# Linear attention followed by a routed expert network: third tiles for the attention, later weights for the second expert, and another order of the steps

## The chip, the core and the metric

The kernel runs on one core of a Trainium2 chip. A core has a matrix engine (PE, with a weight-load queue PEld beside it), a vector engine (DVE), an activation engine (ACT), a general engine (POOL) and a queue engine (SP) that here only issues DMAs. POOL also issues DMAs, among them those that change the number type on the way. The five run their own instruction streams in order and wait for each other by semaphores. The metric is device time in microseconds (us): the median of repeated executions of the whole program, from the inputs in device memory to the output in device memory.

## The reference

```python
def _attn_ref(q, k, v, w_phi):                 # q, k, v: 8 x 8 x 576 x 64
    def phi(x):
        proj = np.einsum('bhsd,df->bhsf', x, w_phi)            # 64 -> 128
        proj = proj - np.max(np.abs(proj), axis=-1, keepdims=True)
        return np.concatenate([np.exp(proj), np.exp(-proj)], axis=-1)
    q_p, k_p = (phi(q), phi(k))
    kv = np.einsum('bhsf,bhsd->bhfd', k_p, v)
    z = np.sum(k_p, axis=2)
    num = np.einsum('bhsf,bhfd->bhsd', q_p, kv)
    den = np.einsum('bhsf,bhf->bhs', q_p, z)[..., None] + 1e-06
    return num / den
# x = the heads side by side: 4608 rows of 512

def _moe_ref(x, w_gate, w1, w2):               # 8 experts, 512 -> 1024 -> 512
    logits = x @ w_gate
    P = np.exp(logits - logits.max())
    for _ in range(8):
        P /= P.sum(1, keepdims=True) + 1e-09
        P /= P.sum(0, keepdims=True) + 1e-09
        P *= N / E
    out = 0
    for e in range(E):
        out += P[:, e:e + 1] * (np.maximum(x @ w1[e], 0.0) @ w2[e])
    return out
```

Every row goes through all eight experts; only the weights P differ by row. P needs the column sums over all 4608 rows, so it can't be formed before the attention is done.

## The kernel before

**Attention.** The eight batches have eight heads each, taken as four pairs of heads, so there are 32 pairs; of each head's 576 rows, 512 are done pair by pair and the last 64 ("rests") for a whole batch at once. A pair goes through four steps. Step a (`pair_a`): the keys stand transposed in a tile `qkT`, PE multiplies them by the small matrix `wphi` (scores), DVE takes the row maxima (`m`, L459), ACT takes the exponentials of both signs (`k0`, `k1`, L463), and POOL scales v by the exponentials of the maxima (`v0`, `v1`, L592). Step q: the same for the queries (`q0`, `q1`). Step b (`pair_b`): PE forms the key-value product, DVE copies it out of PSUM (`kv`, L647), PE multiplies the query features by it in two halves, with a DVE product between them (L678), and DVE divides (reciprocal `rec`, L684, and the products into `xb`, L686 and L691). Step c (`pair_c`): PE transposes `xb` (L705) and DVE copies it into `xT` (L708). Steps r and g do the rests (L479, L525, L720, L725) and the gate's logits of a batch. For the first two batches q and k arrive as 32-bit numbers in the tiles `acc` by way of SP (L389), and PE transposes them (L544); for the others POOL issues a DMA that casts to 16 bits (L395) and SP a DMA that transposes (L412).

**First expert under the attention.** A group is 512 rows of x; there are nine. Step u multiplies a group by two slices of the first expert's `w1` (`up0`, PE L467, ACT evicts with a relu at L759), eight matrix products of 512 columns each. Step d multiplies by `w2` (`down0`), eight products too, and copies into `acc` (L794 on ACT, L801 on DVE). Neither needs P yet, so they fill PE between the attention's short products. Groups 5 to 8 have their `acc` tiles only once the attention's memory has been given back, so their d steps come behind it.

**Handover.** When the last attention tile has been read, the memory of the attention's tiles is released (the plan's key `late`) and used for `acc5` to `acc8`, for the routing and for the experts' sums. DVE then runs eight rounds of the routing (L929 to L946, with a small PE product with `colw` in each round) between the differences of x (`S`, L987) that go out to device memory (`xd`) and come back as `X`. PE meanwhile does what is left of the first expert. When P is there, ACT scales all 36 tiles of the first expert's result by it (L1241).

**The other seven experts** use a scheme with seven products in place of eight on 2 x 2 blocks (PE L1079; ACT L1107, L1116, L1231; DVE L1111, L1219, L987; POOL L1234). Their weights are loaded by POOL (L361) into rings of two tiles each, cast on the way.

**What sets the order.** Nothing is issued directly: every instruction is recorded in a `Plan` with a cost, and a list scheduler places them on the engines, the earliest start first, and among equals the one recorded first. The costs are estimates in `pe`, `act`, `dve`, `pool`, `dma`, the tiles come from rings (`ring(pool, shape, type, name, count)`) and the eight PSUM banks from `Banks`; an instruction can't be placed before a tile of its ring is free. The string `order` gives the order in which the attention's steps are recorded (each letter is the next one of its kind). What the scheduler returns is the order that each engine's stream has on the chip.

Of the kernel before, what the change touches and what calls it, by code (L numbers as in the profile page):

```python
# [9 lines left out]
FP32 = mybir.dt.float32  # L10
# [218 lines left out]
def kernel(  # L229
# [19 lines left out]
    NJ = 4  # L249
# [28 lines left out]
    wgate_f = a_in.tile([128, NP, E], FP32, name="wgate_f")  # L278
# [35 lines left out]
    ring(wp, [128, 4, FF], BF16, "w1", 2)  # L314
    ring(wp, [128, 8, DD], BF16, "w2", 2)
# [11 lines left out]
    ring(a_s, [128, 2, 8], FP32, "m", 2)  # L327
    ring(a_s, [128, 12], FP32, "r", 2)
    ring(a_s, [128, 6], FP32, "rec", 3)
    ring(a_s, [128, NP, 128], BF16, "xb_r", 2)  # L330
    for x in range(2):
        ring(a_t, [128, NP, DF], BF16, f"kr{x}", 2)
        ring(a_t, [128, NP, 128], BF16, f"qr{x}", 2)
        ring(a_t, [128, 8, DF], BF16, f"k{x}", 2)
        ring(a_t, [128, 2, 4, 128], BF16, f"q{x}", 2)
        ring(a_t, [128, 8, D1], BF16, f"v{x}", 2)
        ring(a_s, [128, NP], FP32, f"em_r{x}", 2)
        ring(a_s, [128, 8], FP32, f"em{x}", 2)
# [27 lines left out]
    def load_w0(i, r):  # L366

        w1, w2 = W[0]
        n = i % 4
        if i < 4:  # L370
            dma("POOL", 1 << 19, 250, lambda: nc.gpsimd.dma_start(
                out=w1()[:, :, n * 256:(n + 1) * 256],
                in_=moe_w1[0].rearrange("(c p) f -> p c f", p=128)
                [:, :, n * 256:(n + 1) * 256]), r, [(w1, n)])
        else:
            dma("POOL", 1 << 19, 280, lambda: nc.gpsimd.dma_start(
                out=w2()[:, 2 * n:2 * n + 2, :],
                in_=moe_w2[0].rearrange("(c p) f -> p c f", p=128)
                [:, 2 * n:2 * n + 2]), r, [(w2, n)])

    def load_qk(b, hh, nh, t, r=()):

        o = hh % 4
        keys = [o // 2] if nh == 2 else [0, 1]
        if b < 2:
            g = t["f"]
            for x, src in ((1, k), (0, q)):
                i = 2 * x + o // 2
                dma("SP", nh << 17, 320, lambda x=x, src=src, i=i: nc.sync.dma_start(  # L389
                    out=acc[g][:, i:i + nh // 2].rearrange("p a (h c) -> p (a h) c", h=2),  # L390
                    in_=src[b, hh:hh + nh, 0:SM].rearrange("h (p j) d -> p h (j d)", j=NJ)),
                    r, [("acc", g, 2 * x + n) for n in keys])
            return
        for x, src in ((1, k), (0, q)):
            dma("POOL", nh << 17, 230, lambda x=x, src=src: nc.gpsimd.dma_start(  # L395
                out=t["qk"]()[:, x, o:o + nh],
                in_=src[b, hh:hh + nh, 0:SM].rearrange("h (p j) d -> p h (j d)", j=NJ)),
                r, [(t["qk"], x, i) for i in keys])

    def load_v(b, hh, nh, t, r=()):  # L400
        o = hh % 4
        keys = [o // 2] if nh == 2 else [0, 1]
        dma("SP", nh << 17, 320, lambda: nc.sync.dma_start(
            out=t["v"]()[:, o:o + nh],
            in_=v[b, hh:hh + nh, 0:SM].rearrange("h (p j) d -> p h (j d)", j=NJ)),
            r, [(t["v"], i) for i in keys])
# [24 lines left out]
    def load_rests(b0, nb, r=()):  # L431
# [3 lines left out]
        for h in range(2):  # L435
# [6 lines left out]
            for x, src in ((1, k), (0, q)):  # L442
# [6 lines left out]
                dma("POOL", nb << 16, 90, lambda rows=rows, x=x, src=src, part=part:  # L449
# [19 lines left out]
    def rest_a(b, t):  # L469
# [6 lines left out]
        if b < 2:  # L476
            ptr = new("P1")
            for pr in range(NP):
                pe(128, lambda pr=pr: nc.tensor.transpose(  # L479
# [3 lines left out]
                    [ptr, ("acc", 0, b)])  # L483
# [50 lines left out]
    def pair_a(b, pr, t):  # L534
# [3 lines left out]
        if b < 2:  # L538
            g = t["f"]
            for x in (1, 0):  # L540
                ptr = new("P1")
                i = 2 * x + h0 // 2
                for c in range(4):
                    pe(128, lambda c=c, i=i, ptr=ptr: nc.tensor.transpose(  # L544
                        ptr()[:, c * 128:(c + 1) * 128], acc[g][:, i, c * 128:c * 128 + 128],
                        identf), [("acc", g, i), "identf"], [ptr])
# [75 lines left out]
    def pair_b(b, pr, s, r):  # L622
# [29 lines left out]
        def outs(h):  # L652
# [8 lines left out]
            def feats(x):  # L661
# [3 lines left out]
                for j in range(4):  # L665
# [3 lines left out]
                        skip_group_check=True), keys, [pn])  # L669
# [137 lines left out]
    for b in range(2):  # L807
# [18 lines left out]
    load_qk(0, 4, 4, halves[0, 1])  # L826
    load_v(0, 4, 4, halves[0, 1])
    for i in range(2):
# [4 lines left out]
    dma("SP", 1 << 14, 50, lambda: nc.sync.dma_start(  # L833
        out=wgate_f, in_=moe_w_gate.rearrange("(c p) e -> p c e", p=128)), w=["wgate_f"])
    act(32, lambda: nc.scalar.copy(out=wgate, in_=wgate_f), ["wgate_f"], ["wgate"])

# [29 lines left out]
    def stage_g(b):  # L866
# [8 lines left out]
        "raqaqabbccqaqbbaqrbaccuqrbgaqaquabcucbqccaruqbcabqdaqbacbugdqdaqubdccuubauacuqqd"  # L875
        "drcbagubqbdaqrduabccauqccubqdcbcuadgqgrbuadqbacaudqbqaddcbaurqcuqbcaadubqauabdqd"
        "gbuccdaqdqbdcbqcuuacbgcqcbcg"
# [407 lines left out]
    for e in range(1, E):  # L1285
        w1, w2 = load_w(e, [("xT", 5, 3)])
# [50 lines left out]
```

## Time and profile before

| | |
|---|---|
| median of 3 runs | 1040.92 us (1040.34 to 1041.95) |
| the profiled execution | 1041.77 us, of which the span is 1040.0 us |
| PE busy | 1014.6 us (98%) |
| DVE busy | 821.6 us (79%) |
| ACT busy | 711.6 us (68%) |
| POOL busy | 462.2 us (44%) |
| start, until the first pair's `kv` is copied | 0 to about 21.5 us |
| attention with the first expert under it | to about 216.5 us |
| the rest of the first expert, and the routing | to 259.8 us |
| the seven other experts | to the end |

Times are counted from the first instruction of the span. Busy times of PE, DVE and ACT include the tail of an instruction that overlaps the next one, so back-to-back instructions follow each other more closely than the mean duration of one says. A group's row names the line, the engine, the operation and the tiles with their numbers left out, and behind the bar the idle time of the engine just before these instructions with what ended it.

### The profile page before, as it was taken

The page shows a single profiled execution, that of the slowest core. Times are in us where ns is not written, and L with a number is a line of the kernel's source. Part 1 is how long each engine was busy: PE and PEld are TensorE (multiplying, and loading weights), DVE is VectorE, ACT ScalarE, POOL GpSimd, SP SyncE. Part 2 cuts the span into 40 slices and gives each one's busy share as a digit, 9 for nine tenths or more (in the row PEclk, how much of TensorE's full clock was granted, in tenths as well). Part 3 has the DMA queues.
Part 4 walks back from the last instruction along what each step waited for, and adds up shares of the span by engine and source line. Part 5 has one row for each costly group of instructions (what it writes and reads, how often), then busy time and mean ns, then how long its engine had stood idle before and what let it go on. Part 6 is the DMA issues. An engine that isn't in the chain of part 4 may idle for free.

```text
span 1040.0 us, 24497 instructions
## 1 busy us (share of the span) xinstructions
PE 1014.6 (98%) x9473; PEld 842.0 (81%) x9512; DVE 821.6 (79%) x1626; ACT 711.6 (68%) x1570; POOL 462.2 (44%) x532
## 2 busy tenths in 40 slices
PE   6889999999999999999999999999999999999998
PEld 4556666654788888888888888888888888888886
DVE  6999999988777787778876877788777877787675
ACT  7999999945976666666666665666666656666663
POOL 3886775500234444444434444344444444434442
PEclk9999999999999999999999999999999999999999
DMA  8999979534411161113311441134111611114333
GB/s 240 161 186 144 156 122 173 88 142 112 82 43 51 41 125 50 42 42 83 82 42 42 92 89 45 42 70 99 48 42 48 127 42 42 42 46 128 114 131 122
DMA packets 105237, 93.94 MB, mean 90 GB/s; under 512 B 45344, under 2 KB 80288, under 8 KB 105120
## 3 DMA queue, kind: packets, MB, share of 16 engines
q1 hardware_dynamic: 71840, 68.45, 24.2%
q0 software_dynamic: 33120, 23.86, 16.5%
q8 instruction: 74, 1.21, 0.5%
q14 instruction: 43, 0.35, 0.1%
q10 hardware_dynamic: 160, 0.07, 0.0%
HBM read 94.98 MB, written 14.16 MB: 105 GB/s over the span
## 4 chain that ended last, share of the span: by engine, by line
PE 89%; ACT 3%; DVE 3%; DMA 3%; issue 1%; SPq 0%; DVEq 0%; ACTq 0%
PE P L1079 71%; PE P L467 16%; ACT acc L1241 2%; DMA acc<-in_q_dram 1%; DMA qkT<-qk 1%; PE P L666 1%; DVE m L459 1%; ACT V L1231 1%; PE P L705 1%; ACT U L1107 0%; SPq L389 0%; DVE xb L686 0%; ACT hT L1116 0%; DVE P L678 0%; PE P L671 0%
## 5 line engine op out<-in xcount | busy, mean ns | idle before, releaser
L1234 POOL TENSOR_TENSOR acc<-acc,V 128x512 f32<-128x512 f32 x248 | 317.4, 1287 | 441.0 <-ACT V L1231 437.5
L1111 DVE CUSTOM_DVE_ANT_0 hT<-P,U 128x512 bf16<-128x512 f32 x378 | 255.4, 688 | 129.9 <-ACT U L1107 81.4
L1107 ACT COPY U<-P 128x512 f32<-128x512 f32 x378 | 217.4, 590 | 125.4 <-PE P L1079 120.9
L1231 ACT ACTIVATE V<-P 128x256 f32<-128x256 f32 x496 | 205.8, 476 | 134.7 <-PE P L1079 123.5
L1079 PEld LDWEIGHTS <-w 128*128 128x128 bf16 x2016 | 197.2, 98 | 24.3 <-issue 1.2
L1079 PEld LDWEIGHTS <-S 128*128 128x128 bf16 x1984 | 194.1, 98 | 23.1 <-issue 0.6
L1219 DVE SCALAR_TENSOR_TENSOR acc<-P,acc 128x256 f32<-128x256 f32 x372 | 159.3, 478 | 54.4 <-PE P L1079 51.9
L1079 PEld LDWEIGHTS <-T 128*128 128x128 bf16 x1512 | 147.9, 98 | 18.5 <-issue 1.4
L1079 PEld LDWEIGHTS <-hT 128*128 128x128 bf16 x1488 | 145.4, 98 | 18.2 <-DVE hT L1111 1.1
L1079 PE MATMUL P<-X,w 128*128 128x256 bf16 x1008 | 154.8, 273 | 0.4 <-ACT U L1107 0.4
L1079 PE MATMUL P<-xT,w 128*128 128x256 bf16 x1008 | 151.2, 273 | 0.4 <-ACT acc L794 0.4
L1079 PE MATMUL P<-X,T 128*128 128x256 bf16 x1008 | 148.5, 273 | 0.7 <-ACT U L1107 0.7
L1079 PE MATMUL P<-w,hT 128*128 128x256 bf16 x992 | 142.5, 273 | 0.6 <-DVE hT L1111 0.6
L1079 PE MATMUL P<-T,S 128*128 128x256 bf16 x1056 | 136.3, 273 | 0.4 <-ACT V L1231 0.4
L1079 PE MATMUL P<-w,S 128*128 128x256 bf16 x928 | 126.8, 273 | 0.0
L592 POOL TENSOR_TENSOR v<-v_m,em 128x512 bf16<-128x512 f32 x64 | 66.7, 1042 | 66.1 <-ACT em L463 49.0
L459 DVE TENSOR_REDUCE m<-P 128x4 f32<-128x512 f32 x128 | 83.7, 680 | 4.3 <-PE P L467 2.6
L1116 ACT ACTIVATE hT<-P 128x512 bf16<-128x512 f32 x126 | 73.7, 604 | 12.5 <-PE P L1079 11.9
L987 DVE TENSOR_TENSOR S<-hT 128x1024 bf16<-128x1024 bf16 x124 | 80.2, 683 | 0.0
L467 PE MATMUL P<-w,hT 128*128 128x512 bf16 x301 | 77.6, 379 | 1.2 <-DVE m L459 0.2
L1079 PE MATMUL P<-xT,T 128*128 128x256 bf16 x504 | 75.8, 273 | 0.0
L467 PE MATMUL P<-xT,w 128*128 128x512 bf16 x270 | 73.3, 379 | 1.1 <-DVE m L459 0.2
(94 smaller groups left out, 1088.1 us busy)
## 6 DMA issues: line engine op xcount, KB each, us to landing
X<-xd SPq DMA_DIRECT2D x126, 256.0 KB, 2.6
w<-in_moe_w_dram POOLq DMA_DIRECT2D x14, 1024.0 KB, 10.1
v_m<-in_v_dram SPq DMA_DIRECT2D x15, 512.0 KB, 5.3
out_dram<-acc SPq DMA_DIRECT2D x14, 512.0 KB, 2.9
xd<-S SPq DMA_DIRECT2D x18, 256.0 KB, 2.1
qk<-in_k_dram POOLq DMA_DIRECT2D x12, 256.0 KB, 5.2
qk<-in_q_dram POOLq DMA_DIRECT2D x12, 256.0 KB, 6.2
w<-in_moe_w_dram POOLq DMA_DIRECT2D x8, 256.0 KB, 7.0
```

Of the source, the lines that this page charges most:

```text
L459: dve(el, lambda: nc.vector.tensor_reduce(out=dst(), in_=src(), axis=AX.X, op=ALU.max, apply_absolute_value=True), r, w)
L467: nc.tensor.matmul(out_, lhsT=lhsT, rhs=rhs, start=start, stop=stop)
L592: pool(512, lambda y=y, em=em: nc.gpsimd.tensor_tensor(out=s["v"][y]()[:, :, 0:D], in0=t["v"]()[:, h0:h0 + 2].rearrange("p a (b c) -> p (a ...
L987: lambda: f.tensor_tensor(out=out_(), in0=x(), in1=y(), op=op), r, w, **kw)
L1079: pe(256, lambda i=i, k=k, z=z: nc.tensor.matmul(bank()[:, 256 * i:256 * i + 256], lhsT=lhs(k, i), rhs=rhs(k), start=first and z, stop=k = ...
L1107: act(512, lambda: nc.scalar.copy(out=u[fp][n]().rearrange("p a b -> p (a b)"), in_=x[fp]()), [x[fp]], [u[fp][n]])
L1111: dve(500, lambda: nc.vector._custom_dve(ADD_SAT, out=out_(fp, i, j), in0=bank[fp]().rearrange("p (a b) -> p a b", a=2), in1=u[fp][n](), s ...
L1116: act(512, lambda: nc.scalar.activation(out=out_(fp, i, j), in_=x[fp]().rearrange("p (a b) -> p a b", a=2), func=ACT.Relu, bias=0.0, scale ...
L1219: dve(330, lambda n=n, ts=ts: nc.vector.scalar_tensor_tensor(out=acc[g][:, ts, 256 * j:256 * j + 256], in0=bank()[:, 256 * n:256 * n + 256 ...
L1231: act(390, lambda n=n: nc.scalar.activation(out=u()[:, n, :], in_=bank()[:, 256 * n:256 * n + 256], func=ACT.Copy, bias=0.0, scale=P[:, 4 ...
L1234: pool(670, lambda: nc.gpsimd.tensor_tensor(out=acc[g][:, 2 * i:2 * i + 2, 256 * j:256 * j + 256], in0=acc[g][:, 2 * i:2 * i + 2, 256 * j: ...
L1241: act(512, lambda ts=ts: nc.scalar.activation(out=acc[g][:, ts, :], in_=acc[g][:, ts, :], func=ACT.Copy, bias=0.0, scale=P[:, 4 * g + ts, ...
```

## The change

It has five parts.

1. **Third tiles.** The rings of the attention's tiles `rT`, `qkT`, `kv`, `m`, `r`, `k0`, `k1`, `q0`, `q1`, `v0`, `v1`, `em0`, `em1` have three tiles in place of two, and `xb` four in place of three. The input rings (`qk`, `v_m`, `qk_r`, `v_r`) keep two.
2. **The second weights' place and time.** The second tile of `w1` and of `w2` lies in the memory that the attention gives back. So the weights of the second expert are loaded behind `late`; before, they were loaded once the fourth pair of batch 5 was in `xT`.
3. **Small loads.** The gate's weights are cast by a DMA that POOL issues, in place of a DMA on SP and a cast on ACT. One of the two copies of `w_phi` is loaded by POOL, not ACT. The loads of batch 0's second half are cut in two, in the order k, q, v of heads 4 and 5, then of heads 6 and 7.
4. **The planner's numbers.** DMA rates are lower, the 32-bit transposes are costed at 260 columns in place of 128, and some products take tiles of their rings earlier.
5. **Another string `order`.**

Parts 1, 2, 4 and 5 change no instruction's work; they move instructions. By the two orders, 378 of the first expert's 576 products stood ahead of the last transpose of `xb` on PE before, and 361 stand there now.

The core of the diff:

```diff
@@ -310,33 +310,35 @@
-    ring(wp, [128, 4, FF], BF16, "w1", 2)
-    ring(wp, [128, 8, DD], BF16, "w2", 2)
+    for tag, shape in (("w1", [128, 4, FF]), ("w2", [128, 8, DD])):
+        ring(wp, shape, BF16, tag, 2)
+        R[tag].make = lambda i, w, tag=tag, shape=shape: (late["s_p"] if i else wp).tile(
+            shape, BF16, name=tag, tag=f"{tag}_{i}")
...
-    ring(a_t, [128, NP, 128], BF16, "rT", 2)
-    ring(a_t, [128, 2, 8, 128], BF16, "qkT", 2)
-    ring(a_t, [128, 2, 2, D1], BF16, "kv", 2)
-    ring(a_t, [128, NJ, 128], BF16, "xb", 3)
+    ring(a_t, [128, NP, 128], BF16, "rT", 3)
+    ring(a_t, [128, 2, 8, 128], BF16, "qkT", 3)
+    ring(a_t, [128, 2, 2, D1], BF16, "kv", 3)
+    ring(a_t, [128, NJ, 128], BF16, "xb", 4)
...
-        ring(a_t, [128, 8, DF], BF16, f"k{x}", 2)
-        ring(a_t, [128, 2, 4, 128], BF16, f"q{x}", 2)
-        ring(a_t, [128, 8, D1], BF16, f"v{x}", 2)
+        ring(a_t, [128, 8, DF], BF16, f"k{x}", 3)
+        ring(a_t, [128, 2, 4, 128], BF16, f"q{x}", 3)
+        ring(a_t, [128, 8, D1], BF16, f"v{x}", 3)
...
-            dma("POOL", 1 << 19, 250, lambda: nc.gpsimd.dma_start(
+            dma("POOL", 1 << 19, 200, lambda: nc.gpsimd.dma_start(
...
-                pe(128, lambda pr=pr: nc.tensor.transpose(
+                pe(260, lambda pr=pr: nc.tensor.transpose(
...
-                        True, True), [(t["T"], 0, h0 // 2), "wphi2"], [pt])
+                        True, True), [(t["T"], 0, h0 // 2), "wphi2"], [pt], own)
...
@@ -808,10 +809,9 @@
-    dma("ACT", 1 << 15, 100, lambda: nc.scalar.dma_start(out=wphi_f[0:64, :], in_=w_phi),
-        w=["wphi_f0"])
-    dma("ACT", 1 << 15, 100, lambda: nc.scalar.dma_start(out=wphi_f[64:128, :], in_=w_phi),
-        w=["wphi_f1"])
+    for i, (queue, eng) in enumerate((("ACT", nc.scalar), ("POOL", nc.gpsimd))):
+        dma(queue, 1 << 15, 100, lambda i=i, eng=eng: eng.dma_start(
+            out=wphi_f[64 * i:64 * i + 64, :], in_=w_phi), w=[f"wphi_f{i}"])
...
-    load_qk(0, 4, 4, halves[0, 1])
-    load_v(0, 4, 4, halves[0, 1])
+    for h0 in (4, 6):
+        load_qk(0, h0, 2, halves[0, 1])
+        load_v(0, h0, 2, halves[0, 1])
+    dma("POOL", 1 << 14, 20, lambda: nc.gpsimd.dma_start(
+        out=wgate, in_=moe_w_gate.rearrange("(c p) e -> p c e", p=128)), w=["wgate"])
...
-    dma("SP", 1 << 14, 50, lambda: nc.sync.dma_start(
-        out=wgate_f, in_=moe_w_gate.rearrange("(c p) e -> p c e", p=128)), w=["wgate_f"])
-    act(32, lambda: nc.scalar.copy(out=wgate, in_=wgate_f), ["wgate_f"], ["wgate"])
...
     order = (
-        "raqaqabbccqaqbbaqrbaccuqrbgaqaquabcucbqccaruqbcabqdaqbacbugdqdaqubdccuubauacuqqd"
...
+        "arqaqaqbaqabccbrbqabrcqccaquubaqagbcubcqucuadqgrbabqacqdcbuadabqbuduqccuabauuqcg"
...
-        w1, w2 = load_w(e, [("xT", 5, 3)])
+        w1, w2 = load_w(e, ["late"])
```

What this does to the streams is shown at three places. In the rows a name left of the arrow is what an instruction writes, P is PSUM, and the lines of the changed kernel are off by one or so from those above.

DVE at the start, from the second pair's cast of the transposed keys to the first pair's `kv` copy, before:

```order
L548 CAST qkT<-P 128x512
L484 CAST rT<-P 128x512
L459 TENSOR_REDUCE m<-P 128x4 x2
L459 TENSOR_REDUCE m_r<-P 128x4 x2
L459 TENSOR_REDUCE m<-P 128x4 x2
L548 CAST qkT<-P 128x512 x4
L647 CAST kv<-P 128x260
```

and in the changed kernel:

```order
L549 CAST qkT<-P 128x512
L485 CAST rT<-P 128x512
L460 TENSOR_REDUCE m<-P 128x4
L460 TENSOR_REDUCE m_r<-P 128x4
L460 TENSOR_REDUCE m<-P 128x4
L460 TENSOR_REDUCE m_r<-P 128x4
L460 TENSOR_REDUCE m<-P 128x4 x2
L549 CAST qkT<-P 128x512 x2
L460 TENSOR_REDUCE m<-P 128x4 x2
L549 CAST qkT<-P 128x512 x2
L648 CAST kv<-P 128x260
```

Ahead of the first `kv` copy stand two row maxima (`m`) more, those of the third pair's keys; the casts of the third to sixth pair (`qkT`) stand at the same place.

DVE in the 18th pair's division, from its product with `r` between the two halves to its last `xb`, before:

```order
L678 TENSOR_TENSOR P<-P,r 128x390
L678 TENSOR_TENSOR P<-P,r 128x260
L684 RECIPROCAL rec<-P 128x6
L686 TENSOR_TENSOR xb<-P,rec 128x4x64
L691 TENSOR_TENSOR xb_r<-P,rec 128x128
L684 RECIPROCAL rec<-P 128x4
L686 TENSOR_TENSOR xb<-P,rec 128x4x64
```

and in the changed kernel:

```order
L679 TENSOR_TENSOR P<-P,r 128x390
L679 TENSOR_TENSOR P<-P,r 128x260
L460 TENSOR_REDUCE m<-P 128x4
L685 RECIPROCAL rec<-P 128x6
L460 TENSOR_REDUCE m<-P 128x4
L687 TENSOR_TENSOR xb<-P,rec 128x4x64
L692 TENSOR_TENSOR xb_r<-P,rec 128x128
L685 RECIPROCAL rec<-P 128x4
L648 CAST kv<-P 128x260
L687 TENSOR_TENSOR xb<-P,rec 128x4x64
```

The reciprocal `rec` of six columns reads what PE makes from the product just ahead. Before it stood directly behind the two products; now a row maximum of another pair stands between. Over all 32 pairs the reciprocal stood directly behind the product of 260 columns 11 times, and it does 5 times now.

ACT at the handover, from the last relu of the first expert to the first copies of the second expert's products (`U`), before:

```order
L759 ACTIVATE hT<-P 128x512 x4
L794 ACTIVATE acc_4278<-P 128x512
L1241 ACTIVATE acc_77<-acc_77,P 128x512 x4
L1241 ACTIVATE acc_78<-acc_78,P 128x512
L794 ACTIVATE acc_4279<-P 128x512
L1241 ACTIVATE acc_78<-acc_78,P 128x512 x3
L1241 ACTIVATE acc_79<-acc_79,P 128x512 x3
L794 ACTIVATE acc_4279<-P 128x512
L1107 COPY U<-P 128x512 x2
```

and in the changed kernel, from the fifth scaling on (four stand between the relus ahead):

```order
L1240 ACTIVATE acc_78<-acc_78,P 128x512
L795 ACTIVATE acc_4254<-P 128x512
L1240 ACTIVATE acc_78<-acc_78,P 128x512 x3
L1240 ACTIVATE acc_79<-acc_79,P 128x512 x3
L795 ACTIVATE acc_4255<-P 128x512
L1240 ACTIVATE acc_79<-acc_79,P 128x512
L1240 ACTIVATE acc_80<-acc_80,P 128x512 x4
L1240 ACTIVATE acc_81<-acc_81,P 128x512
L795 ACTIVATE acc_4255<-P 128x512
L1106 COPY U<-P 128x512 x2
```

Ahead of the first `U` copies stood 11 of the 36 scalings by P, and now 17 do.

More of the change, by code (lines that the diff above doesn't have):

```diff
@@ L375, in load_w0 @@
         else:
-            dma("POOL", 1 << 19, 280, lambda: nc.gpsimd.dma_start(
+            dma("POOL", 1 << 19, 225, lambda: nc.gpsimd.dma_start(
                 out=w2()[:, 2 * n:2 * n + 2, :],
@@ L448, in load_rests @@
                     continue
-                dma("POOL", nb << 16, 90, lambda rows=rows, x=x, src=src, part=part:
+                dma("POOL", nb << 16, 100, lambda rows=rows, x=x, src=src, part=part:
                     nc.gpsimd.dma_start(out=t["qk"]()[rows, 0:NP * nb, x, :], in_=part(src)),
@@ L543, in pair_a @@
                 for c in range(4):
-                    pe(128, lambda c=c, i=i, ptr=ptr: nc.tensor.transpose(
+                    pe(260, lambda c=c, i=i, ptr=ptr: nc.tensor.transpose(
                         ptr()[:, c * 128:(c + 1) * 128], acc[g][:, i, c * 128:c * 128 + 128],
-                        identf), [("acc", g, i), "identf"], [ptr])
+                        identf), [("acc", g, i), "identf"], [ptr], [t["T"]])
                 if x:
```

21 lines of the change are left out of this document (10 added, 11 removed).

## The prediction

> **What bounds the kernel now.** I read the page first, then PE's busy time by stages, then the waits of PE and DVE in the stages where PE is not full, then the timelines of the start and of the handover.
>
> ```profile
> span 1040.0 us, 24497 instructions
> ...
> PE 1014.6 (98%) x9473; PEld 842.0 (81%) x9512; DVE 821.6 (79%) x1626; ACT 711.6 (68%) x1570; POOL 462.2 (44%) x532
> ```
>
> Over the whole span PE is the bound. The stages (columns: stretch, its length, busy us and number of instructions of PE, PEld, DVE, ACT, POOL, then PE's granted clock, the share of the DMA engines, GB/s) show where it is not full:
>
> ```profile
> core 0: us, PE busy (x) PEld busy (x) DVE busy (x) ACT busy (x) POOL busy (x), PEclk, DMA share, GB/s
> 259.80:294.82 35.02, 32.41 (x281) 27.14 (x280) 24.41 (x42) 34.97 (x69) 9.70 (x8) 1.00 0.36 76
> 294.82:1028.63 733.81, 733.76 (x6720) 657.63 (x6721) 559.14 (x1002) 460.29 (x960) 315.84 (x252) 1.00 0.26 68
> 216.47:259.80 43.33, 43.10 (x206) 20.62 (x210) 38.65 (x99) 19.44 (x34) 0.82 (x1) 1.00 0.50 152
> 96.00:216.47 120.47, 119.09 (x1373) 79.56 (x1395) 112.06 (x282) 112.23 (x289) 71.98 (x144) 1.00 0.78 126
> 80.00:96.00 16.00, 15.84 (x175) 10.35 (x176) 14.95 (x36) 15.10 (x39) 9.33 (x19) 1.00 1.00 143
> 22.00:80.00 58.00, 50.98 (x602) 34.04 (x609) 54.23 (x137) 54.65 (x145) 44.24 (x88) 1.00 1.16 176
> 0.00:22.00 22.00, 12.61 (x95) 9.69 (x96) 13.77 (x26) 14.87 (x39) 9.28 (x24) 1.00 0.89 239
> ```
>
> From 294.82 on, 71% of the time, PE is full and the change moves nothing that counts. PE loses 9.4 us before 22, 7.0 from 22 to 80 and 2.6 from 259.8 to 294.8 by its busy time. In that last stage the loss is larger, since a waiting product counts as busy: 280 products at the 733.81/6720 = 0.1092 us of the stage behind it are 30.6 us, and it took 35.0, so 4.4 us are lost, with ACT busy for 34.97 of 35.02.
>
> The attention's stage is the subtle one. From 22 to 216.47 DVE is busy for 54.23 + 14.95 + 112.06 = 181.2 of 194.5 us (93.2%) and ACT for 182.0 (93.6%), whether PE is full (96 to 216) or not (22 to 80). PE is filled there with the first expert's products, and what isn't done under the attention is done behind it. So the time follows two things: when the attention ends, set by DVE and ACT, and how many of those products are left then.
>
> **The start.** The rows are of PE, DVE, DVE, DVE and ACT (start, us, what, in brackets the idle time before and what ended it):
>
> ```profile
> 19.29 1.06 PE L544 MATMUL P<-identf,acc 128*128 128x128 f32 x8 [2.01 <-DMA acc<-in_k_dram]
> ...
> 16.89 0.69 DVE L548 CAST qkT<-P 128x512 bf16<-128x512 f32 x1 [1.20 <-PE P L544]
> 19.96 1.29 DVE L548 CAST qkT<-P 128x512 bf16<-128x512 f32 x2 [2.37 <-PE P L544]
> 21.16 0.42 DVE L647 CAST kv<-P 128x260 bf16<-128x260 f32 x1
> ...
> 17.48 0.22 ACT L835 CAST wgate<-wgate_f 128x32 bf16<-128x32 f32 x1 [2.06 <-DMA wgate_f<-in_moe_w_gate_dram]
> ...
> 54.07 2.47 DVE L459 TENSOR_REDUCE m<-P 128x4 f32<-128x512 f32 x4
> ```
>
> PE waits at 19.29 for the keys of batch 1 (`acc2`), and the first pair's key-value products stand behind those transposes, then DVE's `kv` copy. In the new order these transposes stand ahead of the first `kv` as well, so I leave the `kv` copy at 21.16. But two more row maxima stand ahead of it, at (2.47 - 0.68)/3 = 0.60 us each (0.68 is the mean of the group, as of its single rows), in DVE's idle 1.20 and 2.37 us. ACT's wait of 2.06 us for the gate's weights goes; it let the exponentials of the second pair start late, and without it the third pair's can be there in time. **Term 1: -1.2 us.** Ends: -2.4, if four maxima's worth of DVE's 3.57 idle us is filled, and +1.1, if the three SP issues more, less that of the gate's weights, bring the keys of batch 1 later by 2 x 0.55 us (10.47 - 9.92 below):
>
> ```profile
> 9.92 0.51 SPq L833 DMA_DIRECT2D wgate_f<-in_moe_w_gate_dram  x1
> 10.47 1.36 SPq L389 DMA_DIRECT2D acc<-in_k_dram  x1
> 11.87 2.62 SPq L389 DMA_DIRECT2D acc<-in_q_dram  x1
> ...
> acc<-in_k_dram SPq DMA_DIRECT2D x3, 512.0 KB, 4.9
> ...
> acc<-in_k_dram SPq DMA_DIRECT2D x2, 256.0 KB, 3.9
> ```
>
> The last two of SP take 1.36 and 2.62 us to issue, so the queue is already full there, and the bytes ahead are the same; hence I put these keys' landing at no change. The third pair's keys come in a half load now, in 3.9 us from issue where the whole took 4.9 (the last two rows, size and median landing), so they are there for the two maxima. A rule speaks against halves: the Trainium skill, "DMA: Bandwidth & Descriptors", section "Bandwidth", wants loads of 1 MiB or more, a smaller one being ruled by what each costs whatever its size. By that rule the halves bring nothing, half of term 1 goes, and the sum is -2.6. The trace agrees that half the bytes take far more than half the time; that they come earlier all the same decides for me.
>
> `w_phi` by POOL: one copy now waits for POOL's issue and the landing. The first scores start behind both casts:
>
> ```profile
> 3.73 2.01 PE L544 MATMUL P<-identf,acc 128*128 128x128 f32 x8 [3.73 <-DMA acc<-in_k_dram]
> ...
> 5.58 0.22 DVE L820 CAST wphi<-wphi_f 64x128 bf16<-64x128 f32 x1
> ...
> 5.85 1.82 PE L467 MATMUL P<-wphi,qkT 128*128 128x256 bf16 x8
> ...
> qk_r<-in_k_dram POOLq DMA_DIRECT2D x4, 96.0 KB, 5.1
> ...
> wphi_f<-in_w_phi_dram ACTq DMA_DIRECT2D x2, 32.0 KB, 3.4
> ...
> 9.62 1.04 POOL L592 TENSOR_TENSOR v<-v_m,em 128x512 bf16<-128x512 f32 x1 [8.31 <-DMA v_r<-in_v_dram]
> ...
> 251.31 0.82 POOL L361 DMA_DIRECT2D w<-in_moe_w_dram  x1 [42.12 <-PE P L467]
> ```
>
> Issued at about 0.7, as the first loads of the other queues are, it lands 3.4 to 5.1 us later, at 4.1 to 5.8. Both casts now stand ahead of the first `qkT` cast, which takes 0.6 us: scores at 5.5 to 6.8 in place of 5.85. **Term 2: +0.3 us**, ends -0.3 and +1.0, the size being nearer to the small load's row. The identity for the transposes, which POOL makes behind it, comes an issue later, 0.82 us; PE first needs it at 3.73, and waits for the keys until then. The gate's weights cost POOL another 0.82 us under its idle 8.31; if that cover went, each would shift the first `v` by as much.
>
> **The attention.** DVE's waits from 22 to 216:
>
> ```profile
> DVE rec L684 <- PE P L671: 3.0, 8, 0.4
> DVE m L459 <- PE P L467: 1.7, 3, 0.8
> DVE m L459 <- ACT k L463: 1.2, 3, 0.5
> DVE kv L647 <- PE P L467: 1.1, 2, 0.9
> ```
>
> The reciprocals wait 3.0/8 = 0.38 us where nothing stands between them and the product. This was so 11 times in the order and is so 5 times now: six waits, **term 3: -2.3 us**. What the third tiles themselves bring is not in the trace, since a wait for a tile shows as one for its last reader; the nearest row is the 1.2 us of maxima behind ACT's `k` exponentials, and I take that: **term 4: -1.2 us**. Its ends: -5, the table's other waits and as much again of DVE's idle 194.5 - 181.2 = 13.2 us, and +4, if DVE's idle grows by a third in the new order. No instruction is added to DVE or POOL in this stage, and ACT has four relus fewer.
>
> **The products left over.** 17 products fewer stand under the attention, and they go behind it, one by one:
>
> ```profile
> 216.47 4.48 PE L467 MATMUL P<-w,hT 128*128 128x512 bf16 x20
> 220.78 0.28 PE L467 MATMUL P<-cs,colw 128*128 128x8 f32 x2
> ```
>
> (220.78 - 216.47)/20 = 0.2155 us each, **term 5: +3.7 us**, with no range: it is work that PE must do in a stage where it is full (43.10 of 43.33).
>
> **The handover.** ACT after P:
>
> ```profile
> 254.25 3.17 ACT L1241 ACTIVATE acc<-acc,P 128x512 f32<-128x512 f32 x5 [0.88 <-DVE P L946]
> ...
> 257.80 3.77 ACT L1241 ACTIVATE acc<-acc,P 128x512 f32<-128x512 f32 x6
> 261.48 0.57 ACT L794 ACTIVATE acc<-P 128x512 f32<-128x512 f32 x1
> 261.95 1.05 ACT L1107 COPY U<-P 128x512 f32<-128x512 f32 x2
> ```
>
> A scaling takes (261.48 - 257.80)/6 = 0.61 us. With 17 of 36 ahead of the first `U` copy in place of 11, 6 x 0.61 = 3.7 us of ACT work leave the stage in which PE lost 4.4 us to ACT. **Term 6: -2.5 us**, two thirds of it, since a part of PE's waits there is for DVE; ends 0 and -3.7. It needs P early against PE: before, P let ACT go 254.25 - 216.47 = 37.8 us behind the attention, 5.6 ahead of the second expert's first product at 259.80; with 17 products more in between, 9.2 ahead.
>
> The second expert's weights were hidden anyway and stay so: issued at about 212, two loads of 10.1 us at the median and 17.5 at most are there by 247, and their first use is behind P, at 254 now. Without that cover each us late would be a us.
>
> ```profile
> DMA to landing us min/median/max: 8.3/10.1/17.5
> ...
> 254.13 0.68 DVE L987 TENSOR_TENSOR T<-w 128x1024 bf16<-128x1024 bf16 x1
> ```
>
> **Sum:** -1.2 + 0.3 - 2.3 - 1.2 + 3.7 - 2.5 = -3.2 us. Against the profiled execution's 1041.77 us that is 1038.6. That execution lies 0.85 above the median of 1040.92, so for a median I say **1037.7**.
>
> **Rivals.**
> *DVE stays as busy as it is.* If its share holds at 93.2% (for it: the share is alike with and without PE full), the remaining 181.2 - 1.2 = 180.0 us take 193.2, 1.3 less; with terms 2, 5 and 6 the sum is +0.2: 1041.1.
> *The PSUM banks become what is waited for*, and the kernel gets slower. Tiles are tripled, but there are eight banks as before; scores of pairs further ahead hold banks, and PE stands in order behind them. For it: DVE's 1.7 us behind PE's L467 and PE's own waits for maxima. Against it: these are small. Place: 22 to 216. At a share of 91.5% the 180.0 us take 196.8, the sum is +3.8: 1044.7. It decides from 92.3% down, where the attention ends 0.6 us later than now and the sum passes +2.1.
> *The third tiles do more.* At 96% the attention takes 187.5, 6.9 less; the sum is -5.4: 1035.5. For it: the order has the reciprocals covered; against it: PE must then have its share of work done too.
> *The weights collide with the differences.* 18 copies to `xd` and two loads share the DMA engines (0.50 busy there), the ring of five `S` fills, DVE stands, and P is late; at P later by the 9.2 us of its lead term 6 goes and PE loses as much again, 5 us in all: 1042.7.
>
> **Chances.** Forecast 0.50; stronger 0.10; share unchanged 0.15; banks 0.20; collision 0.05. Faster or slower by 0.2% (2.1 us) is about what a measurement tells from no change. Faster takes the first two, 0.60; same most of the third and a bit of the fifth, 0.15; slower 0.25. The range 1033.0 to 1044.0 leaves out the far end of the stronger case and most of the banks' beyond 91.8%; the forecast's own range is 1034.5 to 1039.
>
> **What would show it.** Right: `kv` at about 21 with DVE's idle ahead of it near 2.4; no ACT wait for `wgate`; about five reciprocals that wait; the attention's last product by about 212, the second expert's first product at about 259; ACT's scalings ahead of the first `U` 17; PE's loss in the 35 us behind below 3. Wrong: a DVE share under 92.3% between the first `kv` and the attention's end, scores that wait for maxima more often, or a DVE stop in the differences with the weights in flight.

## The result, and the profile after

The changed kernel takes 1036.87 us (median of 6 runs, 1036.16 to 1038.05) against 1041.22 us before (6 runs, 1040.21 to 1043.16): a ratio of 0.996, with a 95% interval from 0.9948 to 0.9972. The forecast was 1037.7 in a range of 1033.0 to 1044.0. The sum came out nearly right; its terms did not.

The profiled execution of the changed kernel took 1036.16 us, its span is 1034.4. Between the two profiled executions lie 5.6 us, between the medians 4.35, since the one of before lies a little above its median and the one of after below. The page of after:

```profile
span 1034.4 us, 24481 instructions
...
PE 1013.8 (98%) x9476; PEld 843.0 (81%) x9512; DVE 823.7 (80%) x1626; ACT 710.9 (69%) x1569; POOL 462.8 (45%) x534
```

To find the place, both spans are cut at the same four events: the first `kv` copy, the start of the last gate products (end of the attention), the second expert's first product, and the first of PE's last 32 products (in the profile before that one has no record, so the cut there is at the second, one product or 0.22 us later). The windows of before and then of after, with the columns as in the prediction:

```profile
0.00:21.16 21.16, 11.79 (x87) 8.85 (x88) 13.35 (x25) 14.04 (x37) 8.44 (x23) 1.00 0.89 242
21.16:215.39 194.23, 185.72 (x2117) 123.84 (x2151) 180.71 (x452) 182.01 (x471) 126.39 (x250) 1.00 0.91 144
215.39:259.80 44.41, 44.10 (x239) 21.58 (x243) 39.61 (x101) 20.24 (x36) 0.82 (x1) 1.00 0.49 149
259.80:1028.63 768.83, 766.16 (x7001) 684.77 (x7001) 583.54 (x1044) 495.26 (x1029) 325.54 (x259) 1.00 0.27 68
1028.63:1040.00 11.37, 6.85 (x31) 2.94 (x30) 4.43 (x8) 0.00 (x0) 1.00 (x1) 0.93 0.48 184
```

```profile
0.00:19.79 19.79, 13.80 (x91) 9.96 (x91) 14.57 (x27) 14.74 (x38) 8.66 (x23) 1.00 0.97 251
19.79:205.69 185.90, 179.24 (x2098) 122.07 (x2129) 176.44 (x450) 178.15 (x464) 126.40 (x251) 1.00 0.87 139
205.69:253.35 47.66, 47.30 (x255) 22.84 (x259) 40.48 (x101) 25.11 (x45) 2.46 (x3) 1.00 0.74 182
253.35:1022.89 769.54, 766.46 (x7004) 685.06 (x7003) 588.00 (x1044) 492.92 (x1025) 325.27 (x259) 1.00 0.27 68
1022.89:1034.40 11.51, 7.02 (x33) 3.04 (x31) 4.16 (x7) 0.00 (x0) 0.00 (x1) 0.99 0.47 182
```

The start is 1.37 us shorter and the attention 8.33. The rest of the first expert is 3.25 longer; three of its products, 3 x 0.2155 = 0.65 us, stand behind the second expert's first one now and are in the next stage, so it is 3.9 in all. Cut at the same product, the seven experts without these three take 768.89, where they took 768.61: the handover brought nothing. The end is 0.07 shorter. Sum: -1.37 - 8.33 + 3.9 + 0.28 - 0.07 = -5.6.

What the prediction named, read off the trace of after. DVE at the start:

```profile
14.61 1.28 DVE L460 TENSOR_REDUCE m<-P 128x4 f32<-128x512 f32 x2
15.80 1.28 DVE L549 CAST qkT<-P 128x512 bf16<-128x512 f32 x2
17.00 1.28 DVE L460 TENSOR_REDUCE m<-P 128x4 f32<-128x512 f32 x2
18.59 1.29 DVE L549 CAST qkT<-P 128x512 bf16<-128x512 f32 x2 [0.31 <-PE P L545]
19.79 0.42 DVE L648 CAST kv<-P 128x260 bf16<-128x260 f32 x1
```

The two maxima more stand ahead of `kv`, and of DVE's idle time there 0.31 us is left. In the attention DVE and ACT wait like this (two answers of the waits, of DVE and of ACT):

```profile
DVE P L679 <- PE P L672: 1.6, 3, 1.0
DVE m L460 <- PE P L468: 1.1, 3, 0.4
DVE m L460 <- ACT k L464: 1.0, 2, 0.5
...
DVE rec L685 <- PE P L672: 0.6, 2, 0.4
```

```profile
ACT hT L760 <- PE P L468: 2.5, 4, 0.7
...
ACT k L464 <- PE P L468: 0.8, 3, 0.5
```

The reciprocals' waits fell from 3.0 to 0.6 us. At the handover 17 scalings are done ahead of the first `U` copy, as forecast, and yet PE waits (ACT, then PE):

```profile
263.15 3.81 ACT L1240 ACTIVATE acc<-acc,P 128x512 f32<-128x512 f32 x6
266.82 0.61 ACT L1106 COPY U<-P 128x512 f32<-128x512 f32 x1
```

```profile
261.75 0.60 PE L1078 MATMUL P<-X,w 128*128 128x256 bf16 x4 [0.38 <-ACT U L1106]
...
267.48 0.60 PE L1078 MATMUL P<-X,T 128*128 128x256 bf16 x4 [1.33 <-ACT U L1106]
```

Six scalings in a row hold up a `U` copy. Counted as in the prediction (time less products at 0.1092 us), PE loses 4.4 us by 268.6, 15 us into the second expert; before, it lost the same 4.4 over 35 us.

### The profile page after: what moved, and what is told of

Its sections match the earlier page's. It is cut to its first block, busy times and chain, and to the rows that moved or that the text cites. A ratio compares the mean times of both kernels' runs of the same rounds, so it can differ in the third digit from the quotient of the medians.

```text
span 1034.4 us, 24481 instructions
## 1 busy us (share of the span) xinstructions
PE 1013.8 (98%) x9476; PEld 843.0 (81%) x9512; DVE 823.7 (80%) x1626; ACT 710.9 (69%) x1569; POOL 462.8 (45%) x534
## 4 chain that ended last, share of the span: by engine, by line
PE 92%; ACT 4%; DVE 3%; issue 1%; DMA 0%; DVEq 0%; POOLq 0%
PE P L1078 73%; PE P L468 17%; ACT acc L1240 2%; PE P L667 1%; DVE m L460 1%; ACT k L464 1%; PE P L706 1%; ACT q L464 0%; DMA wphi_f<-in_w_phi_dram 0%; DVE xb L687 0%; ACT U L1106 0%; DVE P L679 0%; PE P L672 0%; DVE S L986 0%; DVE m_r L460 0%
## 5 line engine op out<-in xcount | busy, mean ns | idle before, releaser
L986 DVE TENSOR_TENSOR S<-hT 128x1024 bf16<-128x1024 bf16 x124 | 83.4, 709 | 0.3 <-ACT hT L1115 0.3
```

Source lines behind the costliest of these rows:

```text
L986: lambda: f.tensor_tensor(out=out_(), in0=x(), in1=y(), op=op), r, w, **kw)
```

## The experiments

All times stand beside the kernel before on the same chip, in at least five runs. The stages come from one profiled execution each and vary a little: the attention took 185.7 to 186.7 us in five executions with the changed kernel's streams, and the first `kv` copy came between 19.8 and 21.2 us (a profile of experiment 4 had 23.1). The profiled execution took 2.0 to 3.3 us more than the median in experiments 2, 3, 4 and 11, and 1.4 less in experiment 10. In the rows "before" and 11 the experts' stage is cut at the same product as in the others, 0.22 us ahead of the cut in the windows above.

| | median us | ratio to before (95%) | first `kv` | attention | to expert 2 | experts |
|---|---|---|---|---|---|---|
| before | 1041.22 | | 21.16 | 194.23 | 44.41 | 768.61 |
| changed | 1036.87 | 0.9960 (0.9948-0.9972) | 19.79 | 185.90 | 47.66 | 769.54 |
| 1 two tiles | 1048.97 | 1.0075 (1.0062-1.0088) | 20.19 | 202.96 | 43.51 | 768.65 |
| 2 old string | 1047.95 | 1.0066 (1.0053-1.0079) | 21.82 | 202.69 | 44.39 | 768.01 |
| 3 old loads | 1047.36 | 1.0059 (1.0047-1.0072) | 20.46 | 199.07 | 48.31 | 768.76 |
| 4 scalings on POOL | 1049.88 | 1.0079 (1.0067-1.0092) | 23.12 | 186.62 | 58.69 | 771.52 |
| 5 changed again | 1036.71 | 0.9953 (0.9938-0.9968) | 21.20 | 186.68 | 47.66 | 769.52 |
| 6 tiles, old streams | 1039.39 | 0.9986 (0.9975-0.9996) | 19.87 | 194.04 | 44.16 | 768.00 |
| 7 loads, held | 1037.15 | 0.9956 (0.9942-0.9970) | 20.42 | 186.25 | 47.64 | 769.53 |
| 8 scalings later | 1033.73 | 0.9922 (0.9907-0.9938) | 19.98 | 185.73 | 47.67 | 766.80 |
| 9 reciprocals back | 1041.50 | 0.9993 (0.9984-1.0002) | 20.56 | 190.64 | 47.70 | 769.61 |
| 10 one number | 1040.09 | 0.9980 (0.9971-0.9988) | 19.94 | 188.57 | 48.25 | 768.70 |
| 11 before, scalings later | 1039.26 | 0.9976 (0.9967-0.9985) | 20.48 | 196.17 | 44.41 | 766.87 |
| 12 products behind | 1041.40 | 1.0002 (0.9993-1.0011) | 20.58 | 185.22 | 54.13 | 769.54 |

### 1 to 3: one part taken back, the planner free

Experiment 1, the counts of tiles:

```diff
-    ring(a_t, [128, NP, 128], BF16, "rT", 3)
+    ring(a_t, [128, NP, 128], BF16, "rT", 2)
...
```

> The changed kernel with the old counts of tiles (13 rings of two, xb three); loads, string and planner's numbers stay new. The planner then places 382 of the first expert's products under the attention (361 in the changed kernel). Theory 'tiles and string together': without the third tiles DVE waits as it did before; from the first kv copy to the attention's end it needs about 195 us (before 195.3, changed 186.9), so the attention ends 8.4 us later, 21 products of 0.2155 us fewer follow it (4.5 us), and the time is about 1036.9 + 8.4 - 4.5 = 1040.8 us, as before. Rival 'the string and the loads alone': the attention stays as short as in the changed kernel and holds 21 products more in the PE time that is free there; the time is 1036.9 or up to 2 us below.

Experiment 2, the string:

```diff
-        "arqaqaqbaqabccbrbqabrcqccaquubaqagbcubcqucuadqgrbabqacqdcbuadabqbuduqccuabauuqcg"
+        "raqaqabbccqaqbbaqrbaccuqrbgaqaquabcucbqccaruqbcabqdaqbacbugdqdaqubdccuubauacuqqd"
...
```

> The changed kernel with the old string of steps; third tiles, loads and planner's numbers stay new. 377 products stand under the attention. Theory 'tiles and string together': third tiles can't help where the string doesn't record two pairs' work side by side; the attention takes about 193 to 195 us from the first kv copy, the time is 1039.5 to 1041. Rival 'third tiles alone': the attention is about 187 us long, and with 16 products fewer behind it (3.4 us) the time is 1034 to 1037.

Experiment 3, the loads at the start:

```diff
-    for h0 in (4, 6):
-        load_qk(0, h0, 2, halves[0, 1])
-        load_v(0, h0, 2, halves[0, 1])
-    dma("POOL", 1 << 14, 20, lambda: nc.gpsimd.dma_start(
+    load_qk(0, 4, 4, halves[0, 1])
+    load_v(0, 4, 4, halves[0, 1])
...
+    dma("SP", 1 << 14, 50, lambda: nc.sync.dma_start(
+        out=wgate_f, in_=moe_w_gate.rearrange("(c p) e -> p c e", p=128)), w=["wgate_f"])
+    act(32, lambda: nc.scalar.copy(out=wgate, in_=wgate_f), ["wgate_f"], ["wgate"])
...
```

> The changed kernel with the old loads at the start: both w_phi copies by ACT, the gate's weights by SP with a cast on ACT, batch 0's second half unsplit. Theory 'the loads brought the keys of batch 1 earlier': the first kv copy, at 19.79 us in the changed kernel and 21.16 before, goes back to about 21.2, and the time is 1036.9 + 1.4 = 1038.3, or up to 1039.5 if the two more row maxima ahead of it go too. Rival 'the string did it': the kv copy stays below 20.2 and the time within 0.5 us of 1036.9.

All three are slower than the kernel *before*, by 6 to 8 us, and all three in the attention alone: 199 to 203 us. No theory had that. Small loads hardly cost 13 us in the middle of the attention, so the suspicion fell on what the three share: the planner, given other conditions, laid the attention out in another order. The waits of DVE and then of ACT in experiment 1 show how:

```profile
DVE kv L648 <- PE P L468: 6.2, 6, 3.1
DVE P L679 <- PE P L672: 4.0, 6, 1.0
DVE rec L685 <- PE P L672: 3.0, 7, 0.6
```

```profile
ACT hT L760 <- PE P L468: 10.9, 15, 2.5
ACT k L464 <- PE P L468: 6.8, 9, 2.0
```

Both engines wait for PE's scores and key-value products while PE is busy. Over the attention DVE and ACT together wait for PE 10 us in the changed kernel, 17 before, and 38, 39 and 32 in these three (sums of all rows of the waits). For 22.6 of the 37.6 us of experiment 1 PE was at the first expert's products; that their place is the cause was not tried by itself. Two other things add to these attentions. PE's granted clock stood at 0.50 for 3.4, 4.7 and 10.2 us of them, and for none in the profiles of before and after; and in experiment 3 PE stood 3.10 us for a DMA of keys. They are not the whole: two runs of experiment 2 whose mean clock was 1.0 took 1047.3 and 1047.8 us.

So experiments 6, 7, 9 and 12 hold the streams: the planner runs as in the original, and only then tiles, loads or single instructions are changed. In 4, 8 and 11 the planner is free, but the edit leaves its order up to the handover as it was; 10 is a test of the planner itself.

### 4: scalings on POOL

```diff
+                if g >= 4:
+                    pool(670, lambda ts=ts: nc.gpsimd.tensor_tensor(
+                        out=acc[g][:, ts, :], in0=acc[g][:, ts, :],
+                        in1=P[:, 4 * g + ts, 0:1].to_broadcast([128, 512]), op=ALU.mult),
...
```

> The changed kernel with the scalings by P of groups 4 to 8 (20 of 36) on POOL as a product with P spread over 512 columns, in place of ACT. PE loses 4.3 us in the first 15 us of the second expert in the changed kernel, with ACT busy throughout. Theory 'ACT's scalings hold up the U copies': with 16 scalings left on ACT, all ahead of the first U copy, the loss goes below 1.5 us and the time is 1033.4 to 1034.5. Rival 'the loss belongs to the start of an expert' (PE waits for a U copy or an hT that follows its own product closely, whatever else ACT does): the loss stays above 3 us and the time at 1036 to 1038; if POOL's additions then stand behind its scalings, later.

Here the streams up to the handover are those of the changed kernel, and so is the attention. The loss is at the handover, and neither theory holds. Rows of DVE, POOL and PE:

```profile
250.12 11.58 DVE L986 TENSOR_TENSOR w<-w 128x1024 bf16<-128x1024 bf16 x2
```

```profile
250.53 10.01 POOL L1241 TENSOR_TENSOR acc<-acc,P 128x512 f32<-128x512 f32 x10
```

```profile
262.96 1.44 PE L468 MATMUL P<-w,hT 128*128 128x512 bf16 x3 [8.38 <-DVE acc L802]
```

The first of the two DVE instructions, 0.68 us elsewhere, ran from 250.12 to 261.10 while POOL ran ten scalings one behind another (to 260.54), and PE waited 8.38 us for the copy behind them. The clock stood at 0.50 then, from 258.5 to 268.8, and the 13 products behind the wait took 5.64 us in place of 2.80. A rule fits the first part, though no run tests it alone: the Trainium skill, "SBUF — State Buffer", section "Who interferes with whom", has DVE and POOL share one pair of ports that the first to start holds alone. It says so of one instruction; in this trace it lasted through ten, and the DVE instruction waited though its record starts 0.41 us ahead of POOL's first.

### 5 to 7: the parts with the streams held

Experiment 5 is the changed kernel as it is.

> The changed kernel as it is, beside the three runs below. All theories: 1036.5 to 1037.5 us, first kv copy at 19.8 to 20.5, attention 185 to 187 us from there.

It repeats. Experiment 6 is the kernel before with the third tiles, given out after the planner has run, and the second weights behind `late`:

```diff
         done = self.schedule()
+        self.reslot(done, COUNTS)
...
-        w1, w2 = load_w(e, [("xT", 5, 3)])
+        w1, w2 = load_w(e, ["late"])
```

> The kernel before with third tiles (parts 1 and 2 of the change), in which the five streams of the attention are held word for word as they were; only the second expert's weights come behind it. Theory 'third tiles bring nothing unless the streams use them': every tile's last reader is far enough back in the old streams, the attention takes 193.5 to 194.5 us from the first kv copy (before 194.2 to its last gate product), and the time is 1040 to 1041.5. Rival 'the tiles themselves relax waits': 190 us or less, and the time is 1037 or less.

The attention takes 194.04 us, as with two tiles (194.23):

```profile
19.87:213.91 194.04, 186.84 (x2151) 123.81 (x2151) 180.68 (x452) 182.10 (x472) 125.24 (x249) 1.00 0.79 134
```

Third tiles relax nothing in streams made for two. The time is 1.5 to 2 us lower than before all the same: 0.61 in the experts' stage and 0.25 ahead of it, where the later weights moved the streams; the first `kv` copy is 1.3 us earlier, which is within what it varies.

Experiment 7, the old loads with every other instruction held:

```diff
+        b.fn = self.phi
+        for one, two, fn in zip(*self.at_half, self.whole):
+            one.fn = fn
+            two.fn = lambda: None
...
```

> The changed kernel with the old loads at the start, all other instructions held in the order of the changed kernel (in the experiment with the old loads before this one the planner had made another order). Theory 'the loads give 1.4 us': kv copy at 21.2 where the changed kernel has 19.8, attention then as long as in the changed kernel, time 1038.0 to 1038.8. Rival 'the loads are nothing, the streams are all': kv copy below 20.3, time 1036.5 to 1037.5. Rival 'the loads are most of it': 1044 or more, as with the re-planned order, 1047.4.

1037.15 against 1036.71: the loads are worth 0.4 us at most, where the planner's answer to the same loads cost 10 (experiment 3). Whole loads did as well as halves.

### 8 and 11: the scalings spread

```diff
-                    scale=P[:, 4 * g + ts, 0:1]), ["P", ("acc", g, ts)] + akey(g),
+                    scale=P[:, 4 * g + ts, 0:1]), ["P", ("acc", g, ts)] + akey(g)
+                    + ([(hT[0], 0, 0)] if g >= 4 else []),
```

> The changed kernel with the scalings of groups 4 to 8 each held back until ACT and DVE have the group's own hidden values (a tile of hT); the 16 of groups 0 to 3 stay ahead of the first U copy, and the streams up to there are the same. PE loses 4.3 us in the first 15 us of the second expert in the changed kernel, 12 us of it with ACT full. Theory 'ACT's scalings between the U copies make that loss': it falls below 1.5 us, and the scalings 50 to 110 us later cost less than 1 us: 1033.5 to 1035. Rival 'each expert's start loses it whatever ACT does': 1036.5 to 1037.5; worse if the late scalings stand ahead of U copies there.

It is 3.0 us faster than the changed kernel, the fastest of all. ACT (first fence) is no longer full, and PE (second) waits 0.2 to 0.5 us where it waited 1.33. Counted as above, PE loses 1.9 us over 35 us in place of 4.4, not quite the forecast 1.5:

```profile
258.69 1.07 ACT L1106 COPY U<-P 128x512 f32<-128x512 f32 x2 [0.51 <-PE P L1078]
260.22 1.14 ACT L1115 ACTIVATE hT<-P 128x512 bf16<-128x512 f32 x2 [0.45 <-PE P L1078]
263.42 0.84 ACT L1230 ACTIVATE V<-P 128x256 f32<-128x256 f32 x2 [2.05 <-PE P L1078]
```

```profile
261.95 0.39 PE L1078 MATMUL P<-w,hT 128*128 128x256 bf16 x2 [0.24 <-DVE hT L1110]
...
264.31 1.03 PE L1078 MATMUL P<-w,hT 128*128 128x256 bf16 x8 [0.49 <-ACT V L1230]
```

The same edit in the kernel before, from group 3 on:

> The kernel before with the scalings of groups 3 to 8 held back until the group's own hidden values are there; the 11 scalings ahead of the first U copy and all streams up to there are the same. PE loses 4.3 us behind the handover before. Theory 'scalings between the U copies make the loss, not how many stand ahead': it falls by 2 to 3 us as it did in the changed kernel, to 1038 to 1039.2. Rival 'it needs the six more scalings ahead': less than 1 us, 1040.3 to 1041.5.

The experts take 766.87 in place of 768.61, PE's loss falls from 4.4 to 2.7 us, and the time by 2.0 to 2.5, with still 11 scalings ahead. So most of the loss that can go is made by scalings standing between the `U` copies, and it goes without the six more ahead. The stage gains 1.7 us here and 2.7 in experiment 8; what makes that difference was not tried.

### 9: reciprocals directly behind their product

```diff
+            d.insert(j, d.pop(i))
...
```

(DVE's stream alone; `i` is the place of the reciprocal, `j` the one behind the product of 260 columns.)

> The changed kernel with one thing moved on DVE: the reciprocal of six columns stands directly behind the product of 260 columns in all 32 pairs (5 in the changed kernel, 11 before); the streams of the other engines are held. Theory 'term 3': a reciprocal in that place waits 0.27 us on the mean (before: 3.0 us of waits at 11 such places), so 27 more make 7.4 us of DVE waits, the attention takes 193 us from the first kv copy (changed 186), and the time is 1044. Rival 'a wait there takes the place of another': DVE has idle time anyway, the waits rise and others fall, and the time stays at 1036.5 to 1038.5.

```profile
DVE rec L746 <- PE P L731: 6.7, 20, 0.7
```

The waits came nearly as priced: 20 of them, 6.7 us where 0.6 stood before, so 6.1 more. The attention grew by 190.64 - 186.2 = 4.4 us and the time by 4.1 to 4.8, not 7.4. So about 70% of the added waiting (4.4 of 6.1 us, or 0.16 us for each of the 27 places) reached the end; the rest took the place of other waiting.

### 10: one planner's number

```diff
-    dma("POOL", 1 << 14, 20, lambda: nc.gpsimd.dma_start(
+    dma("POOL", 1 << 14, 40, lambda: nc.gpsimd.dma_start(
```

> The changed kernel with one planner's number changed: the rate put down for the DMA of the gate's weights (16 KB) is 40 in place of 20. No instruction changes; the planner lays the attention out anew. Theory 'the new string fits one layout, and another layout of the same work costs what the first three experiments cost': the attention takes 195 us or more, the time is 1044 to 1049. Rival 'the layout is robust and the first three experiments lost by what they took away': the time is within 1 us of 1036.8.

Between the two: 3 us slower than the changed kernel, the attention 2.4 longer (188.57). A number that describes 16 KB of data costs more than half of what the change brought, and all that it does is reorder the streams; the layouts of experiments 1 to 3 cost three to four times as much.

### 12: products moved behind the attention

```diff
+        done = ([o for o in done[:p] if id(o) not in gone and o is not g8] + [g8]
+                + [o for c in chains for o in c]
+                + [o for o in done[p:] if id(o) not in gone and o is not g8])
```

> The changed kernel with the last 16 of the first expert's products that stand under the attention (and their four relus) moved directly behind its last gate product; the order of everything else is held on every engine. 13 of the 16 stood ahead of the last transpose of xb. Theory 'term 5: the attention's length is set by DVE and ACT, and a product left over costs its 0.2155 us': the attention takes the same 186 us from the first kv copy and the time is 1036.8 + 3.4 = 1040.2. Rival 'PE is full there, so a product taken out shortens the attention by what it costs behind it': the attention takes 182.5 to 183.5 us, and the time stays within 0.6 us of 1036.8.

The attention got 1 us shorter, not 3.4, and the time rose by 4.5 to 5 us: term 5's theory holds, and something came on top. Windows of 1 us, and the moved products:

```profile
202.00:203.00 1.00, 0.81 (x15) 0.50 (x13) 1.00 (x5) 0.60 (x1) 0.00 (x0) 1.00 0.00 0
203.00:204.00 1.00, 0.52 (x9) 0.27 (x7) 1.00 (x6) 0.00 (x0) 0.00 (x0) 1.00 0.00 0
204.00:205.00 1.00, 0.48 (x6) 0.36 (x7) 0.96 (x5) 0.00 (x0) 0.00 (x0) 1.00 0.00 0
205.00:206.00 1.00, 0.83 (x16) 0.61 (x16) 0.99 (x4) 0.00 (x0) 0.00 (x0) 0.95 0.00 0
206.00:207.00 1.00, 0.83 (x25) 0.66 (x23) 0.97 (x3) 0.00 (x0) 0.51 (x1) 0.50 0.00 0
...
212.00:213.00 1.00, 1.00 (x4) 0.39 (x3) 0.00 (x0) 0.54 (x1) 0.00 (x0) 0.64 1.10 242
```

```profile
207.14 6.36 PE L505 MATMUL P<-xT,w 128*128 128x512 bf16 x16
```

Without those products PE waited for DVE in the attention's last four us, and then its granted clock stood at 0.50 for some 6 us: the sixteen took 6.36 us in place of 3.45. Runs whose mean clock was 1.0 took 1040.5 to 1040.6, that is 3.7 more than the changed kernel, near the 3.4 of the products; the others bore the clock as well.

## Why the prediction was right, and where it was wrong

The time fell within the range and 0.8 us from the forecast, because two errors of opposite sign partly cancelled, and that is luck: in the profiles the attention with the start gave 5 us more than the terms said, and the handover 2.5 us less. Of the signs that the prediction named, the 17 scalings and the missing wait for `wgate` came. Others did not: two reciprocals waited, not five, `kv` stood at 19.8 with 0.31 us of idle time ahead in place of 21 and 2.4, the second expert began at 253.3 and not 259, and PE's loss behind it was 4.4 us, not below 3.

- **Term 1 (-1.2).** The two maxima moved ahead of `kv` and ACT's wait for the gate's weights went, as said. The first `kv` copy 1.37 us earlier is no proof of it: in other profiles with the old start's streams it came at 19.87 and 20.48. The third pair's maxima needed no halves: with the old loads held in place the time is the same within 0.4 us. The step that half loads come earlier and decide is not borne out. Experiment 7 agrees with the rule weighed there (the Trainium skill, "DMA: Bandwidth & Descriptors", section "Bandwidth", which wants loads of 1 MiB or more) in that the halves brought nothing that could be measured.
- **Term 2 (+0.3).** The first scores began at 6.15 in place of 5.85.
- **Term 3 (-2.3).** The waits went as said (3.0 to 0.6 us), but the whole of them was put on the path. At the share of experiment 9, 4.4 of 6.1 us, they are worth -1.7, an estimate.
- **Term 4 (-1.2).** This step failed. The nearest row, DVE's waits for ACT's `k`, stood for something that isn't there: third tiles alone bring nothing (experiment 6), and that row itself hardly changed (1.2 to 1.0 us). With two tiles the planner made 203 us of the same string, so they may allow an order that two don't; that no order of two tiles is as short was not shown.
- **The attention as a whole.** Forecast for start and attention -4.4 by terms 1 to 4, measured -9.7, of which 1.37 lie within what the first `kv` copy varies. With the price of -1.2 for the maxima moved ahead, which no run tests by itself, and -1.7 for the reciprocals, more than 5 of the 8.3 us in the attention come from other places of the new order. They were not separated, and so the cause of the larger part is shown only as far as the order of the streams. By their sum DVE and ACT wait for PE 7 us less (17 to 10; 12 in experiment 5), and DVE's idle time fell by 4.1 us (13.5 to 9.5). Its busy time fell too, by 4.3 us, of which the two maxima are 1.2: an instruction that has another close behind it overlaps its tail, as a maximum takes 0.68 us alone and 0.60 in a row. So a share of busy time, on which the rivals of the prediction were built, was a poor measure: the busy time is not a constant. The prediction compared the two orders at a few named places (`kv`, the reciprocals), and not how the first expert's products stand between PE's scores all along.
- **Term 5 (+3.7).** Measured 3.9, and experiment 12 shows that it is a real cost at the attention's end and not a mere move: 16 products cost 3.7 us there.
- **Term 6 (-2.5).** This step failed. 17 scalings stood ahead and P was 9.9 us early, both as said; the loss stayed at 4.4 us. The fewer left over did not thin out where it counts: in the first 15 us of the second expert stood 12 of them, six in a row, where 11 had stood, five in a row. The right term was what stands between the `U` copies (experiments 8 and 11).
- **Rivals.** Neither PSUM banks nor the second weights showed as a wait of size; DVE waited once, 1.11 us, for the weights. "Third tiles do more" had the nearest time for the attention's end, 6.9 us earlier where 9.7 came; its mechanism was not the one.

## What to carry to other kernels

Where a list scheduler lays out the work, an experiment that takes back one part tests the scheduler's next answer and not the part: hold the streams, then change one thing. Price a removed wait at less than its length unless the engine is shown to be the path for the whole of it (here some 70% of it counted), and look between the critical copies, not only ahead of them, for work that could wait: spreading 20 scalings was worth 3 us, as much as most of a tuned reordering.

## What the runs showed of the hardware

- PE's clock fell to 0.50 for some 6 us after about four us at 48 to 83% busy, with no idle stretch above 0.79 us (experiment 12). The Trainium skill differs: its page "TensorE: Matmul & The Clock Gate", section "Why this matters for your kernels", asks that PE have no idle gaps above about 3 us, by which nothing would have been lost here. In the profile before, a wait of 2.01 us that ended at 19.29 left the clock at 1.00; in that of experiment 4 the clock fell within a wait of 2.00 us that ended at 20.13, and was 0.50 from 20 to 26.
- With ten POOL products in a row, one DVE product of two bf16 inputs took 10.98 us in place of 0.68 (experiment 4).
- The keys of batch 1 landed between 17.9 and 20.1 us in four profiles with the same loads and streams (after and experiments 4, 5 and 8), which moves the first `kv` copy and all behind it.
